# Two units' keys turned by VectorE and GpSimd instead of by TensorE

## The chip, the cores and the metric

The kernel runs on one core of a Trainium2 chip. The metric is the device time of one execution in microseconds (us); a kernel is told by the median of its runs. Of the profile and the trace, times are microseconds from the first instruction unless marked ns. Engines are called PE (TensorE), DVE (VectorE), ACT (ScalarE), POOL (GpSimd) and SP (SyncE, which here issues transfers).

## The reference

A gated linear attention (4 batches, 8 heads, 768 positions, head size 48) feeds a two-layer network with a squared ReLU (3072 tokens, 384 by 2048 by 384), all in float32.

```python
f = 1.0 / (1.0 + np.exp(-f_logit))
for t in range(S):
    state = f[:, :, t, :, None] * state + np.einsum('bhd,bhe->bhde', k[:, :, t], v[:, :, t])
    y[:, :, t] = np.einsum('bhd,bhde->bhe', q[:, :, t], state)
x = np.ascontiguousarray(attn_out.transpose(0, 2, 1, 3)).reshape(B * S, H * D)
h = x @ w_in
r = np.maximum(h, 0.0)
return (r * r) @ w_out
```

## The kernel before, in words

**Attention.** The 768 positions are cut into 6 blocks of 128 (`TB`), each of two chunks of 64 (`C`). A unit is one pair of heads in one block for all four batches; there are 24, numbered from 0, four to a block: unit 8 is the first of block 2, units 10 and 12 are the third of block 2 and the first of block 3. The fourth unit of a block (11, 15, ...) has no inputs of its own: it works on rows that the other three hand over (`last_kq`, `last_kn`). A unit goes through lettered stages, run by `stage`: `L` loads f, k and q (one tile `fkq`, three tiles in turn), `v` loads the values, `G` is the sigmoid on ACT, `K` scans the gates backwards on DVE and scales the keys, with two small limits on POOL, `Q` scans forwards and scales the queries, `T` turns the keys (tokens to rows) by four PE transposes into a PSUM tile `shared`, and `N` lets ACT copy them to `kn` and a strip of them to `last_kn`. Units 13, 14 and later ones do `B` in the place of `T`: DVE transposes every 32 by 32 block of the keys (`STREAM_TRANSPOSE`), and POOL moves the blocks to their mirrored places by 16 copies; the keys then stand in SBUF and no copy to `kn` is needed.

**Network.** Blocks go through the network in 16 steps each (one per 128 hidden features): `up` is nine PE products into a bank `ph`, `square` is three ACT operations, `rest` a DVE subtraction that gives `gl`, and `down`, two steps later, nine products into three sums `po`. When a block's last `down` is done, `finish` copies the three sums out (ACT, DVE, ACT; `ob`) and SP sends each to DRAM. `flow` runs these steps in one row, numbered n: block 1 in steps 0 to 15, the rest of block 0 in 16 to 25, block 2 from 26.

**What sets the order.** `hook(n, place, ...)` hangs the attention's stages into step n: place 0 is ahead of `up`, 0.5 and 0.7 are around `rest`, 1 is behind `down`. `SLOTS` says after which step a unit's own PE work comes (unit 8: 13, 9: 16, 10: 19, 11: 21, 12: 23, 13: 27), and the tables `STAGE_AT` and `BLOCKS_AT` give the other stages relative to that step. PE, DVE, ACT and SP execute in the order in which the program is written; only POOL's order is chosen by a scheduler when the program is built.

**The slot.** `slot(old, new)` mixes the old unit's outputs with the new unit's scores and state updates on PE. All updates go to the one bank `shared`, the first chunk's (rows 0 to 63) early and the second chunk's (rows 64 to 127) last. Between them stands a tick: a POOL `MEMSET` of one word (`flag`) that waits for the last update of the first chunk, and that the first update of the second chunk waits for:

```python
if c == 0 and b == B - 1 and h:
    seen.append(G.memset(tick, 0).ins)
    behind(seen[0], ins)
elif c and b == 0 and h:
    behind(ins, seen[0])
```

Each engine executes in its own order, so whatever stands ahead of a tick on POOL also stands ahead of the second half of that slot on PE.

Of the kernel before, what the change touches and what calls it, by code (L numbers as in the profile page):

```python
# [13 lines left out]
F32 = mybir.dt.float32  # L14
F32R = mybir.dt.float32r
# [7 lines left out]
P = 128  # L23
B, H, S, D = 4, 8, 768, 48
# [6 lines left out]
NT = B * TB  # L31
# [10 lines left out]

LAG = 2
Q = 32
TURNED = 13
AHEAD = 4
LO = 6
SPLIT = 2
# [9 lines left out]

SLOTS = (13, 16, 19, 21, 23, 27, 31, 35, 39, 43, 47, 51, 55, 59, 63, 67, 71)
STAGE_AT = ((-6, 0, "Lv"), (-3, 1, "GK"), (-1, 0.5, "Q"), (-1, 1, "TN"), (1, 1, "s"))  # L60
BLOCKS_AT = ((-6, 0, "Lv"), (-3, 1, "GKB"), (-1, 0.5, "Q"), (0, 0.7, "N"), (1, 1, "s"))
LAST_AT = ((-6, 0, "v"), (1, 1, "s"))


# [291 lines left out]
    return t.rearrange("p (n t) -> p n t", t=C)  # L356


def scanned(t):
    return t.rearrange("p (n t) -> p n t", t=CZ)  # L360


def fast_path(ctx, psum, tc, moe, ident, low, flag, fkqT, vN, w, w4, out):
    nc = tc.nc
    V, G = nc.vector, nc.gpsimd
# [17 lines left out]
    for r in (0, C):  # L383
        G.affine_select(
            out=mask[r : r + C], in_=mask[r : r + C], compare_op=ALU.is_ge, fill=0.0,
# [19 lines left out]
    class Unit:  # L405
# [36 lines left out]
        def gates(self):  # L442
            nc.scalar.activation(scanned(self.fz[:, 1:])[:, :, :C], chunks(self.ft), AF.Sigmoid)  # L443

        def keys(self):

            rr = self.rr
            V.tensor_tensor_scan(  # L448
                out=rr[:, ::-1], data0=self.fz[:, NZ * CZ : 0 : -1], data1=dr[:, ::-1], initial=0.0,
                op0=ALU.mult, op1=ALU.add,  # L450
            )
            for pe, of in ((self.pe, rr[:, ::CZ]), (low[:, self.t], self.pe)):
                G.tensor_scalar(out=pe, in0=of, scalar1=LOWEST, scalar2=None, op0=ALU.max)  # L453
            V.tensor_tensor(
                out=chunks(self.kt), in0=chunks(self.kt), in1=scanned(rr)[:, :, 1:], op=ALU.mult
            )
# [54 lines left out]
                    out=self.pk[:, b], in_=self.kt[:, b * TB : (b + 1) * TB], identity=ident  # L511
                )

        def turn_blocks(self):


            if self.n < 14:
                both = self.wk([P, 2, NT], "ys")
                kb, kn = both[:, 0], both[:, 1]
            else:  # L520
                kb, kn = (
                    moe.gp.tile([P, NT], F32, tag=f"part{i}", name=f"turn{self.nm}_{i}", bufs=1) for i in range(2)
                )
            V.transpose(out=kb, in_=self.kt)  # L524
            kb, self.kn = (t.rearrange("p (b n) -> p b n", b=B) for t in (kb, kn))
            self.pk = self.kn
            for a in range(0, P, Q):
                for r in range(0, P, Q):
                    G.tensor_copy(out=self.kn[a : a + Q, :, r : r + Q], in_=kb[r : r + Q, :, a : a + Q])  # L529

        def turned(self):
            if self.n < TURNED:
                self.kn = self.wk([P, B, ROWS], "kn")
                nc.scalar.copy(out=self.kn, in_=self.pk[:, :, :ROWS])
            at = self.hp * (C - D)
            nc.scalar.copy(
                out=last_kn.rearrange("p b (h r) -> p b h r", h=2)[:, :, :, at : at + C - D],
                in_=self.pk.rearrange("p b (h r) -> p b h r", h=2)[:, :, :, D:],
            )
# [100 lines left out]
        def upper(self):  # L640

            self.x = self.xs[self.blk]
            y = self.x[self.hp] if self.own else self.wk([ROWS, 2, NT], "ys", 1, F32R)
            if not self.own:
                self.x.append(y)
            self.y = [y[:ROWS, i].rearrange("p (b c t) -> p c b t", b=B, c=NC) for i in range(2)]
            self.py = self.py[:ROWS].rearrange("p c (b t) -> p c b t", t=C)
            nc.scalar.copy(out=self.y[0], in_=self.py)  # L648
# [26 lines left out]
        def stage(self, letters):  # L675
            for c in letters:
                {
                    "L": lambda: self.load(slice(0, 3)),
                    "f": lambda: self.load(slice(0, 1)),
                    "k": lambda: self.load(slice(1, 2), slice(2, 3)),  # L680
                    "v": lambda: self.load_v(),
                    "G": lambda: self.gates(),
                    "K": lambda: self.keys(),
                    "Q": lambda: self.queries(),
                    "m": lambda: self.move(),
                    "r": lambda: self.crossed(),
                    "T": lambda: self.turn(),
                    "B": lambda: self.turn_blocks(),
                    "N": lambda: self.turned(),
                    "D": lambda: self.add(),  # L690
                    "S": lambda: self.scores(),
                    "M": lambda: self.masked(),
                    "C": lambda: self.states(),
                    "s": lambda: self.crossed_states(),
                    "Y": lambda: self.outputs(),
                    "H": lambda: self.upper(),
                    "z": lambda: self.less(),
                    "X": lambda: self.lower(),
                    "g": lambda: self.parts((1,), G if self.blk < 2 else nc.sync),
                    "h": lambda: self.parts((0,), nc.sync),  # L700
                }[c]()
# [7 lines left out]
    )  # L709
    half = list(range(LO)), list(range(LO, NF))  # L710
    xs = {blk: moe.new_x(blk, blk) for blk in range(2)}
    units, decoding, shared = {}, {}, []

    for t in xs[0]:
        G.memset(t[C + 32 :].bitcast(F32), 0.0)
# [10 lines left out]
    def slot(old, new):  # L726

        ab = ps_a.tile([P, 2, 512], F32, tag="ab", name=f"ab{(new or old).nm}_{new is None}")
        rows = [[], []]
        if old:
            old.py = ab[:, :, : B * C]
            for c in range(NC):
                for b in range(B):
                    for part in range(2):
                        for h in (c, 1 - c):
                            rows[c].append((C, lambda a=(part, b, c, h): old.output_one(*a)))
        if new:  # L740
            new.sd = ab[:, :, B * C :]
            new.dd = shared[0].rearrange("p (c e) n -> p c (e n)", c=NC)[:, :, : B * D]
            adds = [
                [] if new.last_of(c) else [
                    (D, lambda a=(b, c, h): update(*a)) for b in range(B) for h in (c, 1 - c)
                ] for c in range(NC)
            ]
            for h in range(2):
                for b in range(B):
                    for c in (h, 1 - h):  # L750
                        rows[h].append((C, lambda a=(b, c, h): new.score_one(*a)))
            rows = [adds[0] + rows[0], rows[1] + adds[1]]
        seen = []

        def behind(ins, first):
            tc.add_manual_dep(ins, first.name, mybir.DependencyInfo(
                mybir.DependencyClass.Sync, mybir.DependencyReason.DATA
            ), reason="one bank")

        def update(b, c, h):  # L760
            ins = new.add_one(new.dd, b, c, h).ins
            if c == 0 and b == B - 1 and h:

                seen.append(G.memset(tick, 0).ins)  # L764
                behind(seen[0], ins)
            elif c and b == 0 and h:
                behind(ins, seen[0])

        at = [0, 0]
        while any(rows):  # L770
            r = min((r for r in range(2) if rows[r]), key=lambda r: at[r])
            cols, do = rows[r].pop(0)
            at[r] += cols
            do()
# [51 lines left out]
    with tc.manual_schedule(engines={ET.PE, ET.SP, ET.DVE, ET.Activation}):  # L826
# [21 lines left out]
        def hook(n, at, do):  # L848
            hooks.setdefault((max(n, 0), at), []).append(do)

        def third():
            early.close()
            moe.inputs(ctx)
            xs[2] = moe.new_x(2, 2)

# [3 lines left out]
        for n in range(1, NF - 1):  # L861
# [23 lines left out]
            hook(n, 0.5, after)  # L885
            hook(n, 0.7, last)
        hook(NF - 1, 0, third)
        late = [Unit(n, xs, (ps_a,)) for n in range(2 * HP, NBLK * HP)]
        for at, old, un in zip(SLOTS, (None, *late), (*late, None)):
            if un:  # L890
                for n, place, stage in LAST_AT if not un.own else STAGE_AT if un.n < TURNED else BLOCKS_AT:
                    hook(at + n, place, lambda un=un, stage=stage: un.stage(stage))
            hook(at, 1, lambda old=old, un=un: slot(old, un))
            if old:
                hook(at, 1, lambda old=old: old.stage("HX" if old.own else "HXhg"))
            if un:
                hook(at, 1, lambda un=un: un.stage("rMCm" if un.own else "rMC"))
# [238 lines left out]
```

## Time and profile before

| | |
|---|---|
| median of 3 runs | 483.72 us (483.42 to 485.64) |
| profiled execution | 485.02 us, of which the span from first to last instruction is 483.2 |
| granted PE clock, mean | 0.985 of full speed |
| PE busy | 467.4 us, 97% of the span |
| ACT, DVE, POOL busy | 277.7, 261.8 and 80.0 us |
| PE, four transposes of one late unit | line L510, into `shared`, 16 of them (units 8, 9, 10, 12) |

"Busy" is the share of the span in which an engine executes; PE's products are pipelined, so the distance from one start to the next is the better measure of what a product costs. A line such as L244 is line 244 of the kernel before. In a timeline, equal instructions that follow each other are merged into one row with their count, and a bracket tells how long the engine was idle and what ended that.

### The profile page before, as it was taken

Reading aid. Unit: us, or ns where it says so; the run is one execution under the profiler, and the core shown is the slowest. Engines: PE = TensorE matmul, PEld = TensorE weight load, DVE = VectorE, ACT = ScalarE, POOL = GpSimd, SP = SyncE. Lnnn points to the kernel's source line nnn. Section 1 sums busy time; section 2 is a strip of 40 time slices with the busy share of each in tenths; the row PEclk is TensorE's granted clock in tenths of the full one; section 3 lists DMA queues with packets and bytes.
Section 4 is the critical chain, followed back from the end, with each engine's and each line's share of the span. In section 5 each row is a group of like instructions: output and inputs, shape, how many; then the busy total and the mean of one; then the engine's idle time right before and its main releaser. Section 6 shows DMA issues by size and latency. Waiting matters only on the chain. (4 is left out here: it accounts for less than half of the span.)

```text
span 483.2 us, 11552 instructions
## 1 busy us (share of the span) xinstructions
PE 467.4 (97%) x4763; PEld 384.8 (80%) x4763; DVE 261.8 (54%) x482; ACT 277.7 (57%) x562; POOL 80.0 (17%) x210
## 2 busy tenths in 40 slices
PE   5889999999999999999999999999999999999996
PEld 4767788888888888888888888888888888888884
DVE  7998885889966557543447453356353312221111
ACT  4687666877857565545546645555654543544441
POOL 6122010001010004150053250052350000000000
PEclk8699999999999999999999999999999999999999
DMA  8985316568104205332005332004300002100002
GB/s 290 308 248 139 102 41 228 170 208 288 32 14 157 84 3 125 95 94 81 3 2 125 96 93 84 1 1 111 108 12 3 2 0 34 66 0 2 1 0 71
DMA packets 22636, 42.60 MB, mean 88 GB/s; under 512 B 4512, under 2 KB 8128, under 8 KB 22576
## 3 DMA queue, kind: packets, MB, share of 16 engines
q1 hardware_dynamic: 22128, 40.86, 27.8%
q0 software_dynamic: 448, 0.92, 0.8%
q8 instruction: 39, 0.64, 0.5%
q14 instruction: 21, 0.17, 0.1%
HBM read 31.69 MB, written 4.72 MB: 75 GB/s over the span
## 5 line engine op out<-in xcount | busy, mean ns | idle before, releaser
L244 PE MATMUL ph<-x,w 128*128 128x512 f32 x864 | 214.9, 393 | 0.0
L244 PEld LDWEIGHTS ph<-x,w 128*128 128x128 f32 x864 | 160.0, 188 | 34.2 <-DVE gl L261 0.3
L271 PE MATMUL po<-gh,w 128*128 128x512 f32 x570 | 175.5, 389 | 0.0
L261 DVE TENSOR_TENSOR gl<-ph,gh 128x512 fp32r<-128x512 f32 x95 | 65.4, 688 | 158.8 <-ACT gh L256 158.6
L254 ACT ACTIVATE ph<-ph 128x512 f32<-128x512 f32 x96 | 55.9, 582 | 125.2 <-PE ph L244 124.9
L271 PEld LDWEIGHTS po<-gh,w 128*128 128x128 f32 x570 | 107.0, 188 | 22.2
L271 PE MATMUL po<-gl,w 128*128 128x512 f32 x285 | 111.1, 390 | 0.0
L271 PEld LDWEIGHTS po<-gl,w 128*128 128x128 f32 x285 | 53.5, 188 | 11.2
L255 ACT ACTIVATE ph<-ph 128x512 f32<-128x512 f32 x96 | 55.9, 582 | 3.0
L256 ACT CAST gh<-ph 128x512 fp32r<-128x512 f32 x95 | 55.8, 587 | 3.0
L529 POOL COPY turn<-turn 32x128 f32<-32x128 f32 x112 | 42.1, 376 | 8.3 <-DVE turn L524 3.7
L453 POOL TENSOR_SCALAR fkq<-fkq 128x8 f32<-128x8 f32 x18 | 12.9, 717 | 144.9 <-DVE fkq L448 122.1
L448 DVE TENSOR_TENSOR_SCAN fkq<-fz,dr 128x520 f32<-128x520 f32 x18 | 22.3, 1238 | 7.2 <-ACT fz L443 7.2
L169 ACT CAST w<-wa 128x384 fp32r<-128x384 f32 (+1 forms) x33 | 16.6, 513 | 15.4 <-DVE wa L156 11.7
L462 DVE TENSOR_TENSOR_SCAN fkq<-fz,dz 128x520 f32<-128x520 f32 x18 | 22.4, 1246 | 0.6
L619 PE MATMUL ab_False<-sc,vn 64*48 64x64 f32 (+1 forms) x480 | 20.7, 220 | 0.0
L141 ACT ACTIVATE wa<-raw 128x384 f32<-128x384 f32 (+1 forms) x33 | 18.1, 549 | 4.0 <-DMA raw<-in_w_dram 3.9
L664 DVE TENSOR_TENSOR x<-ab_False,x 112x512 fp32r<-112x512 f32 x12 | 8.3, 692 | 21.7 <-ACT x L648 21.7
L648 ACT CAST x<-ab_False 112x512 fp32r<-112x512 f32 x12 | 7.0, 587 | 22.5 <-PE shared L554 17.6
L628 PE MATMUL ab_False<-rx,sx 48*48 48x64 f32 (+1 forms) x240 | 19.4, 216 | 0.0
L764 POOL MEMSET flag<- 1x1 int32 x16 | 1.4, 88 | 106.2 <-PE shared L554 104.3
L152 DVE SCALAR_TENSOR_TENSOR wa<-raw,wa 128x384 int32<-128x384 int32 (+1 forms) x33 | 18.0, 552 | 0.7
(148 smaller groups left out, 494.0 us busy)
## 6 DMA issues: line engine op xcount, KB each, us to landing
raw<-in_w_dram SPq DMA_DIRECT2D x32, 384.0 KB, 4.2
fkq<-in_fkqT_dram SPq DMA_DIRECT2D x15, 768.0 KB, 5.9
vn<-in_vN_dram SPq DMA_DIRECT2D x24, 192.0 KB, 4.7
out_dram<-ob SPq DMA_DIRECT2D x14, 256.0 KB, 2.2
fkq<-in_fkqT_dram SPq DMA_DIRECT2D x9, 256.0 KB, 4.8
x<-ys SPq DMA_DIRECT2D x30, 64.0 KB, 2.4
last_kq<-fkq SPq DMA_DIRECT2D x28, 64.5 KB, 2.3
out_dram<-part SPq DMA_DIRECT2D x3, 256.0 KB, 2.2
```

The costliest lines, as they stand in the source:

```text
L141: nc.scalar.activation(a, upper_f, AF.Abs, scale=2.0**-112, **kw)
L244: self.nc.tensor.matmul(self.cur.ph[f], lhsT=w[:, i], rhs=x[:, j], start=first and n == 0, stop=last and n == 2)
L254: nc.scalar.activation(ph, ph, AF.Relu)
L255: nc.scalar.activation(ph, ph, AF.Square)
L256: nc.scalar.copy(out=gh, in_=ph)
L261: self.nc.vector.tensor_tensor(out=gl, in0=self.cur.ph.pop(f), in1=gh.bitcast(F32), op=ALU.subtract)
L271: self.nc.tensor.matmul(c.po[e], lhsT=l, rhs=r, start=f == c.fs[0] and i == 0, stop=f in c.ends and i == 2, skip_group_check=len(c.ends) > 1,)
L448: V.tensor_tensor_scan(out=rr[:, ::-1], data0=self.fz[:, NZ * CZ : 0 : -1], data1=dr[:, ::-1], initial=0.0, op0=ALU.mult, op1=ALU.add,)
L462: V.tensor_tensor_scan(out=pp, data0=self.fz[:, : NZ * CZ], data1=dz, initial=0.0, op0=ALU.mult, op1=ALU.add)
L529: G.tensor_copy(out=self.kn[a : a + Q, :, r : r + Q], in_=kb[r : r + Q, :, a : a + Q])
L619: nc.tensor.matmul(to[:m], lhsT=self.vn[rows, b, h * D : h * D + m], rhs=self.sc[rows, h, b], start=b == 0, stop=none and c == 0 and b == ...
L628: nc.tensor.matmul(to[:m], lhsT=s[rows, b * D : b * D + m], rhs=q[rows], start=False, stop=b == B - 1,)
```

## The change

Units 10 and 12 now turn their keys by DVE's block transpose and POOL's 16 copies as the later ones do; only units 8 and 9 still use PE in this part. `turn_blocks` is split into `blocks` (`b`, the DVE transpose) and `turn_blocks` (`B`, the POOL copies). Unit 10 writes into the tile that will later hold the third input row group of block 2 (`x2`), unit 12 into `ys`. Unit 10's other stages stay where they were. Unit 12 gets a table of its own, `EARLY_AT`: its load moves from place 0 to place 1 of step 17, and its sigmoid and keys move up from step 20 to step 18; its copies come after slot 19. The copies are told to the scheduler as standing behind the tick of the slot before them.

```diff
-BLOCKS_AT = ((-6, 0, "Lv"), (-3, 1, "GKB"), (-1, 0.5, "Q"), (0, 0.7, "N"), (1, 1, "s"))
+BLOCKS_AT = ((-6, 0, "Lv"), (-3, 1, "GKbB"), (-1, 0.5, "Q"), (0, 0.7, "N"), (1, 1, "s"))
+EARLY_AT = (
+    (-6, 1, "Lv"), (-5, 1, "GKb"), (-4, 1, "B"), (-1, 0.5, "Q"), (0, 0.7, "N"), (1, 1, "s")
+)
...
-        def turn_blocks(self):
+        def blocks(self):
...
             if self.n < 14:
-                both = self.wk([P, 2, NT], "ys")
-                kb, kn = both[:, 0], both[:, 1]
+                kb, kn = halved(
+                    self.wk([P, 2, NT], "ys") if self.blk > 2 else
+                    moe.xs[2].tile([P, 2, NT], F32, tag="x2", name=f"turn{self.nm}")
+                )
...
             V.transpose(out=kb, in_=self.kt)
-            kb, self.kn = (t.rearrange("p (b n) -> p b n", b=B) for t in (kb, kn))
+            self.kb, self.kn = (t.rearrange("p (b n) -> p b n", b=B) for t in (kb, kn))
             self.pk = self.kn
+
+        def turn_blocks(self):
+
             for a in range(0, P, Q):
                 for r in range(0, P, Q):
-                    G.tensor_copy(out=self.kn[a : a + Q, :, r : r + Q], in_=kb[r : r + Q, :, a : a + Q])
+                    ins = G.tensor_copy(
+                        out=self.kn[a : a + Q, :, r : r + Q], in_=self.kb[r : r + Q, :, a : a + Q]
+                    ).ins
+                    for t in ticks[-1:]:
+                        tc.add_manual_dep(ins, t.name, mybir.DependencyInfo(
+                            mybir.DependencyClass.NoSync, mybir.DependencyReason.SCHED_ONLY
+                        ), reason="behind the last slot")
 
         def turned(self):
-            if self.n < TURNED:
+            if self.n < 10:
...
+        def stages_of(un):
+            if not un.own:
+                return LAST_AT
+            return STAGE_AT if un.n < 10 else EARLY_AT if un.n == 12 else BLOCKS_AT
```

What that makes of the order is seen at three places. Line numbers are those of the kernel shown, so the same code has a higher number in the changed kernel; `fkq_2`, `turn_2` belong to unit 10, `fkq_0`, `ys_0` to unit 12.

**POOL, around slot 19, before.** The first `MEMSET` is the tick of slot 16, the next that of slot 19, the last two those of slots 21 and 23.

```order
L764 MEMSET flag 1x1
L453 TENSOR_SCALAR fkq_2_1763<-fkq_2_1763 128x8
L453 TENSOR_SCALAR low<-fkq_2_1763 128x8
L764 MEMSET flag 1x1
L453 TENSOR_SCALAR fkq_0_2033<-fkq_0_2033 128x8
L453 TENSOR_SCALAR low<-fkq_0_2033 128x8
L764 MEMSET flag 1x1 x2
```

The same place in the changed kernel:

```order
L785 MEMSET flag 1x1
L460 TENSOR_SCALAR fkq_2_1763<-fkq_2_1763 128x8
L460 TENSOR_SCALAR low<-fkq_2_1763 128x8
L541 COPY turn_2_2031<-turn_2_2031 32x4x32 x16
L460 TENSOR_SCALAR fkq_0_2085<-fkq_0_2085 128x8
L460 TENSOR_SCALAR low<-fkq_0_2085 128x8
L785 MEMSET flag 1x1
L541 COPY ys_0_2125<-ys_0_2125 32x4x32 x16
L785 MEMSET flag 1x1 x2
```

Unit 10's copies and unit 12's two limits on its keys now stand ahead of the tick of slot 19.

**SP, steps 16 to 21, before.** These are the transfers that SP issues, in order: the rows handed over by units 8 and 9, the load of unit 12, the three outputs of block 1, the rows of unit 10.

```order
L473 DMA last_kq<-fkq_1_1632 16x1032 x2
L436 DMA fkq_0_2033<-in_fkqT_dram 128x3x512
L440 DMA vn_0_2035<-in_vN_dram 128x384
L336 DMA out_dram<-ob_0_2062 128x512
L336 DMA out_dram<-ob_1_2065 128x512
L336 DMA out_dram<-ob_2_2068 128x512
L473 DMA last_kq<-fkq_2_1763 16x1032 x2
```

The same place in the changed kernel:

```order
L480 DMA last_kq<-fkq_1_1632 16x1032 x2
L338 DMA out_dram<-ob_0_2074 128x512
L338 DMA out_dram<-ob_1_2077 128x512
L338 DMA out_dram<-ob_2_2080 128x512
L443 DMA fkq_0_2085<-in_fkqT_dram 128x3x512
L447 DMA vn_0_2087<-in_vN_dram 128x384
L480 DMA last_kq<-fkq_2_1763 16x1032 x2
```

The load of unit 12 moved behind the three outputs.

**DVE, steps 17 to 19, before.** Each scan stands here as `SCALAR_TENSOR_TENSOR` (in the trace `TENSOR_TENSOR_SCAN`); `ob_1` is the second output copy.

```order
L448 SCALAR_TENSOR_TENSOR fkq_2_1763<-fz_71,dr 128x520
L454 TENSOR_TENSOR fkq_2_1763<-fkq_2_1763 128x512
L261 TENSOR_TENSOR gl_7_2048<-ph_7_2037,gh_7_2047 128x512
L335 COPY ob_1_2065<-po_0_1_1320 128x512
L460 RECIPROCAL dz<-fkq_2_1763 128x8
L462 SCALAR_TENSOR_TENSOR fkq_2_1763<-fz_71,dz 128x520
L465 TENSOR_TENSOR fkq_2_1763<-fkq_2_1763 128x512
L261 TENSOR_TENSOR gl_8_2084<-ph_8_2073,gh_8_2083 128x512
L261 TENSOR_TENSOR gl_9_2122<-ph_9_2111,gh_9_2121 128x512
```

The same place in the changed kernel:

```order
L461 TENSOR_TENSOR fkq_2_1763<-fkq_2_1763 128x512
L533 STREAM_TRANSPOSE turn_2_2031<-fkq_2_1763 128x512
L263 TENSOR_TENSOR gl_7_2060<-ph_7_2049,gh_7_2059 128x512
L337 COPY ob_1_2077<-po_0_1_1320 128x512
L467 RECIPROCAL dz<-fkq_2_1763 128x8
L469 SCALAR_TENSOR_TENSOR fkq_2_1763<-fz_71,dz 128x520
L472 TENSOR_TENSOR fkq_2_1763<-fkq_2_1763 128x512
L263 TENSOR_TENSOR gl_8_2100<-ph_8_2089,gh_8_2099 128x512
L455 SCALAR_TENSOR_TENSOR fkq_0_2085<-fz_72,dr 128x520
L461 TENSOR_TENSOR fkq_0_2085<-fkq_0_2085 128x512
L533 STREAM_TRANSPOSE ys_0_2125<-fkq_0_2085 128x512
L263 TENSOR_TENSOR gl_9_2138<-ph_9_2127,gh_9_2137 128x512
```

Unit 10's transpose came in ahead of the output copy `ob_1`, and unit 12's keys came in ahead of `gl_9`. On ACT the sigmoid of unit 12 now stands behind `gh_8`, ahead of the ReLU of step 19, and the two copies to `kn` are gone.

## Rows read from the trace of the kernel before

**Rows 1.** Page, busy time, share of the span and instructions of each engine.

```profile
PE 467.4 (97%) x4763; PEld 384.8 (80%) x4763; DVE 261.8 (54%) x482; ACT 277.7 (57%) x562; POOL 80.0 (17%) x210
```

**Rows 2.** Timeline of PE, end of step 18: start us, us, instruction, count.

```profile
150.18 0.39 PE L271 MATMUL po<-gl,w 128*128 128x512 f32 x1
...
152.26 0.60 PE L510 MATMUL shared<-ident,fkq 128*128 128x128 f32 x4
152.61 2.33 PE L244 MATMUL ph<-x,w 128*128 128x512 f32 x9
154.78 0.39 PE L271 MATMUL po<-gl,w 128*128 128x512 f32 x1
```

**Rows 3.** Timeline of PE, second half of slot 19, steps 20 and 21.

```profile
158.34 0.20 PE L554 MATMUL shared<-vn,kn 64*48 64x48 f32 x1
...
161.01 0.39 PE L271 MATMUL po<-gl,w 128*128 128x512 f32 x1
...
163.05 2.20 PE L244 MATMUL ph<-x,w 128*128 128x512 f32 x9
165.09 0.39 PE L271 MATMUL po<-gl,w 128*128 128x512 f32 x1
```

**Rows 4.** Timeline of PE, transposes of unit 12.

```profile
173.35 0.60 PE L510 MATMUL shared<-ident,fkq 128*128 128x128 f32 x4
173.70 2.31 PE L244 MATMUL ph<-x,w 128*128 128x512 f32 x9
```

**Rows 5.** Timeline of DVE: unit 10's keys, output copy, a scan, unit 13's transpose.

```profile
148.69 0.69 DVE L454 TENSOR_TENSOR fkq<-fkq 128x512 f32<-128x512 f32 x1
...
149.90 0.68 DVE L335 COPY ob<-po 128x512 f32<-128x512 f32 x1
...
164.48 1.24 DVE L448 TENSOR_TENSOR_SCAN fkq<-fz,dr 128x520 f32<-128x520 f32 x1 [0.74 <-ACT fz L443]
...
187.56 0.71 DVE L524 STREAM_TRANSPOSE ys<-fkq 128x512 f32<-128x512 f32 x1
188.20 0.69 DVE L261 TENSOR_TENSOR gl<-ph,gh 128x512 fp32r<-128x512 f32 x1
```

**Rows 6.** Timeline of SP's issues: load of unit 12, second and third output.

```profile
143.59 0.60 SPq L436 DMA_DIRECT2D fkq<-in_fkqT_dram  x1
...
150.61 0.81 SPq L336 DMA_DIRECT2D out_dram<-ob  x2
```

**Rows 7.** DMA view, loads issued at 158.45, 210.86, 143.59, 115.87; last column: us to landing.

```profile
fkq<-in_fkqT_dram SPq DMA_DIRECT2D x1, 768.0 KB, 4.8
...
fkq<-in_fkqT_dram SPq DMA_DIRECT2D x1, 768.0 KB, 4.6
...
fkq<-in_fkqT_dram SPq DMA_DIRECT2D x1, 768.0 KB, 6.4
...
fkq<-in_fkqT_dram SPq DMA_DIRECT2D x1, 768.0 KB, 8.2
```

**Rows 8.** Timeline of ACT: a unit's sigmoid.

```profile
163.82 0.63 ACT L443 ACTIVATE fz<-fkq 128x512 f32<-128x512 f32 x1
```

**Rows 9.** Timeline of POOL: tick of slot 19, unit 12's limits, unit 13's copies.

```profile
157.58 0.09 POOL L764 MEMSET flag<- 1x1 int32 x1 [7.78 <-PE shared L554]
165.81 0.74 POOL L453 TENSOR_SCALAR fkq<-fkq 128x8 f32<-128x8 f32 x1 [8.14 <-DVE fkq L448]
166.63 0.23 POOL L453 TENSOR_SCALAR low<-fkq 128x8 f32<-128x8 f32 x1
...
188.41 6.74 POOL L529 COPY ys<-ys 32x128 f32<-32x128 f32 x16 [0.47 <-DVE ys L524]
```

**Rows 10.** Windows: us, busy us of each engine (instructions), PEclk, DMA share, GB/s.

```profile
8.10:21.70 13.60, 10.44 (x209) 8.67 (x213) 12.95 (x21) 8.78 (x23) 3.76 (x8) 0.50 1.05 347
...
38.00:42.00 4.00, 2.98 (x71) 2.29 (x70) 3.67 (x6) 2.79 (x6) 0.95 (x2) 1.00 0.22 42
```

**Rows 11.** Timeline of PE, first transposes of the program.

```profile
7.42 0.66 PE L510 MATMUL pk<-ident,fkq 128*128 128x128 f32 x4 [2.36 <-DVE fkq L454]
```

More of the change, by code (lines that the diff above doesn't have):

```diff
@@ L44 @@
 Q = 32
-TURNED = 13
 AHEAD = 4
@@ L356, in chunks, with halved @@
     return t.rearrange("p (n t) -> p n t", t=C)
+def halved(t):
+    t = t.rearrange("p a n -> p (a n)")
+    return t[:, :NT], t[:, NT:]
 def scanned(t):
@@ L642, in upper @@
             self.x = self.xs[self.blk]
+            if self.blk == 2 and self.own:
+                self.x.append(moe.xs[2].tile([P, 2, NT], F32R, tag=f"x{self.hp}", name=f"x2_{self.hp}"))
             y = self.x[self.hp] if self.own else self.wk([ROWS, 2, NT], "ys", 1, F32R)
@@ L687, in stage @@
                     "T": lambda: self.turn(),
+                    "b": lambda: self.blocks(),
                     "B": lambda: self.turn_blocks(),
@@ L711, in fast_path @@
     xs = {blk: moe.new_x(blk, blk) for blk in range(2)}
-    units, decoding, shared = {}, {}, []
+    units, decoding, shared, ticks = {}, {}, [], []
     for t in xs[0]:
@@ L764, in update @@
                 seen.append(G.memset(tick, 0).ins)
+                ticks.append(seen[0])
                 behind(seen[0], ins)
@@ L853, in third @@
             moe.inputs(ctx)
-            xs[2] = moe.new_x(2, 2)
+            xs[2] = []
         hook(0, 0.5, rest_of_first)
@@ L888, in fast_path @@
         late = [Unit(n, xs, (ps_a,)) for n in range(2 * HP, NBLK * HP)]
+        def stages_of(un):
+            if not un.own:
+                return LAST_AT
+            return STAGE_AT if un.n < 10 else EARLY_AT if un.n == 12 else BLOCKS_AT
         for at, old, un in zip(SLOTS, (None, *late), (*late, None)):
             if un:
-                for n, place, stage in LAST_AT if not un.own else STAGE_AT if un.n < TURNED else BLOCKS_AT:
+                for n, place, stage in stages_of(un):
                     hook(at + n, place, lambda un=un, stage=stage: un.stage(stage))
```

## Prediction

> **What bounds the kernel now.** I read the page's busy times first, then PE's timeline step by step. PE is busy for 97% of the span, no other engine for more than 57% [rows 1], so the question at every edit is what it takes from PE and whether PE has to wait for it. PE's starts then show how tightly it runs: from one `down` to the next `up` and on to the next `down` are 2.04 us each (161.01 to 163.05 to 165.09), nine products with no hole [rows 3]. In steps 16 to 23, where the change lies, PE waits for nothing. So PE's own work there is worth its full length, and any new wait costs its full length too. The slots are the only places in this part where PE depends on POOL: the second chunk's updates of slot 19 start at 158.34 [rows 3], and the tick that they need was written at 157.58 [rows 9], after 7.78 us in which POOL did nothing but wait for PE.
>
> **What is removed.** Unit 10's four transposes stand between 152.26 and 152.61: 0.35 us. The `up` behind them takes 2.17 (to 154.78), 0.13 more than the plain 2.04, and the `down` ahead of them 2.08 (150.18 to 152.26), 0.04 more [rows 2, 3]. Together 0.52 us. Unit 12's stand from 173.35 to 173.70, again 0.35 [rows 4]; with the same 0.13 behind them that is 0.48. Sum: 1.00 us off PE. The bound below it is the bare 0.70, if the slower neighbours have another cause. The two copies to `kn` go from ACT, which is not what PE waits for, and count nothing.
>
> **What is added off the path.** Two DVE transposes of 0.71 each, with the next instruction 0.64 after [rows 5], and twice 16 POOL copies, 6.74 per unit [rows 9]. Unit 10's: its scaled keys end at 149.38 (148.69 + 0.69), the transpose would start at 149.42 and end at 150.13, the copies run from about 150.3 to 157.0. The first chunk's updates need only the eight copies into rows 0 to 63, which are done before 156.4, where slot 19 will now begin; the second chunk's come at 157.8. So these copies stay hidden, but with 0.8 us to spare: if they were that much later they would stall PE directly. Unit 12's copies come behind the tick of slot 19 and have until slot 23. The two tiles lent for the blocks are written again only after slots 21 and 23, behind the updates that read them; that costs nothing while PE's order holds.
>
> **What is moved, and whom it makes wait.** Unit 12's load now stands on SP behind the three outputs, and unit 12's two limits stand on POOL ahead of the tick of slot 19. That ties slot 19 to a load. I follow it through.
>
> The second output waits for DVE's copy `ob_1`, which started at 149.90 and ended at 150.58 [rows 5]; SP issued it at 150.61 [rows 6]. With unit 10's transpose ahead of it, keys end 149.38, transpose from 149.42, `gl_7` from 150.06, `ob_1` from 150.66 to 151.34. SP issues outputs two and three from 151.37 and needs 0.81 us for both [rows 6], so unit 12's load goes out at about 152.2; before, it went out at 143.59 [rows 6].
>
> A load of this size (768 KB) that ran alone landed 4.8 and 4.6 us after its issue; the one issued at 143.59 took 6.4, and one issued at 115.87, beside the weight loads, 8.2 [rows 7]. I take 4.8, since the outputs ahead are short and nothing else is under way: it lands at 157.0.
>
> The sigmoid takes 0.63 [rows 8], to 157.65. The scan starts then; POOL's first limit starts 1.33 us after the start of a scan (164.48 to 165.81), the second 0.82 later, and that one lasts 0.23 [rows 5, 9]. So the first starts at 159.0, the second ends at 160.1, and the tick is written at about 160.2, where PE would be ready for it at 157.82 (158.34 less the 0.52 gained). PE waits about 2.4 us in the middle of slot 19. Behind the stopped update on PE stand the rest of slot 19 and everything after it, so nothing covers this.
>
> Sum: + 2.43 - 1.00 = + 1.4 us. With the load at 4.6 us it is + 1.2; at 6.4 us, + 3.0; at 8.2 us, + 4.8; with the transposes at their lower bound 0.3 more.
>
> For the load there is a rule: the Trainium skill, "DMA: Bandwidth & Descriptors", section "Anatomy of one DMA", puts a transfer at a fixed 2.0 us plus its bytes over 436 GB/s, by its own account fitted for another issuing path. For 768 KB that is an estimate of 3.8 us, by which the wait would be 1.4 and the sum + 0.4. The trace does not bear it out, since the two loads alone took 4.6 and 4.8 [rows 7].
>
> What is late next: ACT has the sigmoid ahead of the ReLU of step 19, which would start at 157.7. Its `gl_9` would then end by 161.2, and PE needs that bank for the `up` of step 21, which starts only after 165. DVE's and POOL's following work has as much room. I count no second wait.
>
> **The forecast.** The profiled execution took 485.02 us and would take 486.4; the median of the runs lies 1.30 below that execution. 483.72 + 1.43 gives 485.2 us, 0.3% slower. About 0.5% (2.4 us) is what a measurement of this kernel can tell from no change, so I count this as within it.
>
> **The rivals.**
>
> A: PE's wait costs the clock. The granted clock was 0.50 from 8.1 to 21.7 us [rows 10], and shortly before it fell PE had stood idle for 2.36 us, until 7.42 [rows 11]; the wait that I expect is as long. Against it: between 38 and 42 us PE was busy for only 2.98 of 4 us, and the clock stayed at 1.00 [rows 10]; and unlike at the start, dense products stand before and behind this wait. At half clock, PE loses half of the stretch: 6.8 us if it lasted 13.6 us as it did there, but then PE was fed poorly; with its work at hand I take a quarter to a half of that, 1.7 to 3.4. It decides from 1.0 us on, since 1.4 + 1.0 passes the bound. The time would be 486.9 to 488.6. The Trainium skill, "TensorE: Matmul & The Clock Gate", section "Why this matters for your kernels", warns of idle gaps between bursts of products in the middle of a kernel for this reason. The trace agrees for the gap at the start and shows no such gap later.
>
> B: the load is slow. The three outputs' bytes are still moving when it is issued, or something else is. At 6.4 to 8.2 us to landing [rows 7] the time is 486.7 to 488.5. Against it: outputs are a third of its size each and nothing else is due.
>
> C: PE does not wait, and only the removed transposes count: 483.72 - 1.0 = 482.7 us. That asks for a tick at 157.8, so for a load that lands at 154.6, 2.4 us after its issue. Nothing of this size came near that [rows 7]; it could happen only if SP issued the load 2.4 us sooner than I work out, so if `ob_1` were not late and the outputs went out at once.
>
> **How the numbers follow.** The forecast gets 0.52 (its own range is 484.9 to 486.1, loads of 4.6 to 5.5 us), A 0.28, B 0.08, C 0.10, a gain past 2.4 us by something that I do not see 0.02. Within 0.5% are the forecast and C, 0.62, less 0.03 for a wait at its upper end: 0.59. Slower are A, B and that end: 0.39. The range leaves out C below and the ends of A and B above: 484.4 to 488.6.
>
> **What would show it.** In the changed kernel's trace: `up` directly behind `down` at the ends of steps 18 and 22, with 2.04 us each; unit 12's load issued at about 152.2, landing near 157; the sigmoid waiting for that landing; POOL's two limits behind the scan, then the tick; and in the wait view a PE wait for POOL's `flag` of about 2.4 us in slot 19, a single one. Wrong would be: no such wait (C), a wait of more than 3.5 us (B), a granted clock of 0.50 in the slices behind slot 19 (A), or a wait at the start of slot 19 for the copies, or at the `up` of step 21 for `gl_9`.

## The result and the profile after

The changed kernel takes 487.49 us (median of 6 runs, 486.71 to 488.03), the kernel before 483.69 beside it (6 runs, 483.38 to 485.64): a ratio of 1.0068, 95% interval 1.0054 to 1.0082. It is slower, by 0.68% as that ratio has it (3.3 us); the two medians differ by 3.8 us. I had forecast 1.4 us and "within 0.5%". The time lies in my range and in the intervals of rivals A and B.

The profiled execution took 488.03 us, with a span of 486.3. PE is busy 1.2 us longer than before [rows 1], although 8 of its 4763 instructions are gone; POOL is busy 11 us longer. The page:

```profile
PE 468.6 (96%) x4755; PEld 384.9 (79%) x4755; DVE 263.2 (54%) x484; ACT 277.3 (57%) x560; POOL 91.0 (19%) x242
```

I measure the change by one stretch, from the first product of slot 16 to the first of slot 27, since the edit lies inside it. It is 54.43 us long before (142.01 to 196.44) and 57.13 after (141.95 to 199.08): 2.70 more. The rest agrees to 0.06 up to the start of the last `down`; from there to the end it took 13.02 us before and 13.43 after. That 0.4 us belongs to the change too: the tail is 13.0 in the kernel before and in those below with one unit turned (e2, e3), and 13.4 to 13.5 in all eleven traces with both. All of it lies behind the last output copy, where the program closes (3.20 us before, 3.62 after); what takes it there stays open. Below I compare the stretch; the tail comes on top of it.

The view of PE's waits names two in this stretch, where before there was none:

```profile
PE shared L572 <- POOL flag L785: 2.7, 1, 2.7
PE po L273 <- DVE ob L337: 0.3, 1, 0.3
```

Columns are us in total, times, and the longest. PE's timeline shows both in place, and answers to [rows 2, 3]:

```profile
150.12 0.39 PE L273 MATMUL po<-gl,w 128*128 128x512 f32 x1
150.35 0.61 PE L273 MATMUL po<-gh,w 128*128 128x512 f32 x2
151.30 0.50 PE L273 MATMUL po<-gl,w 128*128 128x512 f32 x1 [0.34 <-DVE ob L337]
...
152.80 2.21 PE L246 MATMUL ph<-x,w 128*128 128x512 f32 x9
154.84 0.39 PE L273 MATMUL po<-gl,w 128*128 128x512 f32 x1
...
161.39 0.25 PE L572 MATMUL shared<-vn,turn 64*48 64x48 f32 x2 [2.68 <-POOL flag L785]
161.90 2.37 PE L246 MATMUL ph<-x,w 128*128 128x512 f32 x9
164.10 0.40 PE L273 MATMUL po<-gl,w 128*128 128x512 f32 x1
```

From the top: the `down` of step 18 stops before its second sum, and lasts 2.68 us (150.12 to 152.80) instead of 2.08. The `up` behind it starts with no transposes between and takes 2.04. In slot 19 the second chunk's updates wait 2.68 us for the tick; the slot, which began at 156.97, lasts 4.92 us to the `up` at 161.90, where it had lasted 1.92. That is 3.00 more, since the trace counts a wait from the end of the product ahead, and products overlap. So the stretch is +0.60 + 3.00 - 0.95 (what the transposes gave back), about +2.7.

The long wait is followed back through the other engines' timelines and the issue view. POOL, where the tick is the `MEMSET` [rows 9]:

```profile
150.21 6.66 POOL L541 COPY turn<-turn 32x128 f32<-32x128 f32 x16 [0.47 <-ACT sx L490]
160.40 0.59 POOL L460 TENSOR_SCALAR fkq<-fkq 128x8 f32<-128x8 f32 x1 [3.54 <-DVE fkq L455]
161.07 0.23 POOL L460 TENSOR_SCALAR low<-fkq 128x8 f32<-128x8 f32 x1
161.25 0.09 POOL L785 MEMSET flag<- 1x1 int32 x1
161.77 5.47 POOL L541 COPY ys<-ys 32x128 f32<-32x128 f32 x16 [0.43 <-DVE ys L533]
```

DVE [rows 5] and ACT [rows 8]:

```profile
149.36 0.71 DVE L533 STREAM_TRANSPOSE turn<-fkq 128x512 f32<-128x512 f32 x1
150.00 0.65 DVE L263 TENSOR_TENSOR gl<-ph,gh 128x512 fp32r<-128x512 f32 x1
150.57 0.68 DVE L337 COPY ob<-po 128x512 f32<-128x512 f32 x1
...
158.93 1.24 DVE L455 TENSOR_TENSOR_SCAN fkq<-fz,dr 128x520 f32<-128x520 f32 x1 [4.79 <-ACT fz L450]
```

```profile
158.26 0.63 ACT L450 ACTIVATE fz<-fkq 128x512 f32<-128x512 f32 x1 [6.13 <-DMA fkq<-in_fkqT_dram]
```

SP's issues [rows 6], and from the DMA view the load of unit 12 with its us to landing [rows 7]:

```profile
148.90 3.20 SPq L338 DMA_DIRECT2D out_dram<-ob  x3
152.20 0.62 SPq L443 DMA_DIRECT2D fkq<-in_fkqT_dram  x1
152.86 0.64 SPq L447 DMA_DIRECT2D vn<-in_vN_dram  x1
153.60 1.15 SPq L480 DMA_DIRECT2D last_kq<-fkq  x2
```

```profile
fkq<-in_fkqT_dram SPq DMA_DIRECT2D x1, 768.0 KB, 6.0
```

Read backwards: the tick at 161.25 stands behind the two limits, these behind the scan of 158.93, that behind the sigmoid of 158.26, that behind a load issued at 152.20. POOL had its 16 copies done at 156.87 and then waited 3.54 us with the tick in its queue, although the first chunk's updates, which alone the tick needs, were done by 158.71, when PE fell idle.

### The profile page after: what moved, and what is told of

It is laid out like the page before. It is cut to its first block, busy times and chain, and to the rows that moved or that the text cites. A ratio compares the mean times of both kernels' runs of the same rounds, so it can differ in the third digit from the quotient of the medians.

```text
span 486.3 us, 11573 instructions
## 1 busy us (share of the span) xinstructions
PE 468.6 (96%) x4755; PEld 384.9 (79%) x4755; DVE 263.2 (54%) x484; ACT 277.3 (57%) x560; POOL 91.0 (19%) x242
## 5 line engine op out<-in xcount | busy, mean ns | idle before, releaser
L246 PEld LDWEIGHTS ph<-x,w 128*128 128x128 f32 x864 | 160.2, 188 | 35.0 <-DVE w L173 0.8
L541 POOL COPY turn<-turn 32x128 f32<-32x128 f32 x128 | 48.3, 377 | 9.7 <-DVE turn L533 4.0
```

The source lines that it names most:

```text
L246: self.nc.tensor.matmul(self.cur.ph[f], lhsT=w[:, i], rhs=x[:, j], start=first and n == 0, stop=last and n == 2)
L541: ins = G.tensor_copy(out=self.kn[a : a + Q, :, r : r + Q], in_=self.kb[r : r + Q, :, a : a + Q]).ins
```

## The experiments

The theories: **T1**, the loss is PE's waits, one for the load through limits and tick, one for the output copy behind unit 10's transpose. **T2**, the turning on DVE and POOL costs PE time by itself. **T3** (rival A), the idle of slot 19 lowers PE's clock behind it. All are read on the same stretch, 54.43 us before. Ratios are to the kernel before on the same chip.

### e1: the load of unit 12 ahead of the outputs

```diff
-    (-6, 1, "Lv"), (-5, 1, "GKb"), (-4, 1, "B"), (-1, 0.5, "Q"), (0, 0.7, "N"), (1, 1, "s")
+    (-6, 0, "Lv"), (-5, 1, "GKb"), (-4, 1, "B"), (-1, 0.5, "Q"), (0, 0.7, "N"), (1, 1, "s")
```

> Only the load of unit 12 goes back to place 0 of step 17, ahead of the three outputs. If the wait in slot 19 comes from that load by way of the two limits ahead of the tick (the main theory), the load lands at about 150, the limits are done right behind unit 10's copies at 158.0, and PE waits 0 to 0.2 us there in place of 2.68; what is left is +0.6 us for the output copy that comes late to the down of step 18 and -1.0 us for the eight transposes: 483.3 us. If the rival holds (POOL is simply late with unit 10's 16 copies, slowed by DVE), the load changes nothing: a wait of about 2.7 us and 486.5 us or more.

484.51 us, ratio 1.0014 (0.9998 to 1.0029); stretch 54.57. The load was issued at 143.03 and landed at 147.88, and of the long wait 0.16 us was left, in a slot of 2.40; the `down` of step 18 stayed at 2.68. That is T1, with one surprise that made it 0.5 us longer than I expected. POOL:

```profile
149.71 7.94 POOL L541 COPY turn<-turn 32x128 f32<-32x128 f32 x16 [0.47 <-ACT sx L490]
157.73 0.24 POOL L460 TENSOR_SCALAR fkq<-fkq 128x8 f32<-128x8 f32 x1
158.05 0.23 POOL L460 TENSOR_SCALAR low<-fkq 128x8 f32<-128x8 f32 x1
158.23 0.09 POOL L785 MEMSET flag<- 1x1 int32 x1
```

The 16 copies now take 7.94 us instead of 6.66, and limits and tick come right behind them. Most single copies take 0.29 us; one that meets a scan of DVE takes 1.1 to 1.2, and the next, which meets the scaling behind the scan, 0.75. With unit 12's keys early, a second scan runs beside the copies. The Trainium skill, "SBUF — State Buffer", section "SBUF: two separate sides", says why: VectorE and GpSimd share one pair of SBUF ports, held for a whole instruction, also by a VectorE instruction with two SBUF inputs. The trace agrees: the copy that met unit 12's scan ended at 154.87, the scan at 154.78.

### e2 and e3: one unit alone

e2 leaves unit 10 to PE, e3 unit 12.

e2:

```diff
-            if self.n < 10:
+            if self.n < 11:
...
-            return STAGE_AT if un.n < 10 else EARLY_AT if un.n == 12 else BLOCKS_AT
+            return STAGE_AT if un.n < 11 else EARLY_AT if un.n == 12 else BLOCKS_AT
```

e3:

```diff
-            if self.n < 10:
+            if self.n < 10 or self.n == 12:
...
-            return STAGE_AT if un.n < 10 else EARLY_AT if un.n == 12 else BLOCKS_AT
+            return STAGE_AT if un.n < 10 or un.n == 12 else BLOCKS_AT
```

> Unit 10 is turned by PE again; unit 12 stays as in the change, its load behind the outputs. Main theory: the tick still stands behind the limits that wait for the load, which goes out 0.7 us sooner (no DVE transpose ahead of the output copy), so PE waits about 2.2 us in slot 19; no 0.6 us in step 18; -0.5 us for unit 12's transposes: 485.4 us. Rival (unit 10's copies hold the tick): no copies, no wait, 483.2 us.

> Unit 12 is back as before (PE transposes, load and keys in their old places); unit 10 as in the change. Main theory: no limits of unit 12 ahead of the tick, so no wait in slot 19 beyond 0.2 us; the down of step 18 still takes about 0.6 us more since the output copy stands behind unit 10's DVE transpose; -0.5 us for unit 10's transposes: 483.8 us, no change. Rival (copies): the wait of 2.7 us stays and the time is about 486.4 us.

e2: 487.39 us, ratio 1.0054 (1.0031 to 1.0076). No wait in step 18, and a wait of 1.75 us in slot 19, which lasted 3.99. But the stretch is 57.71, not some 56: behind that wait PE's clock fell. Columns of a window: us, busy us of PE, PEld, DVE, ACT and POOL with their instructions, granted clock, DMA share, GB/s.

```profile
161.50:164.90 3.40, 3.40 (x10) 2.64 (x9) 2.32 (x6) 1.53 (x4) 2.98 (x11) 0.50 0.35 132
```

The `up` there took 3.13 us and the `down` 2.73, 1.65 us over the usual 2.17 and 2.04. Without that it would be 56.06, as expected. That was the first sign of T3, and behind an idle shorter than the 2.68 of the changed kernel's first trace, where the clock had stayed.

e3: 484.13 us, ratio 1.0004 (0.9992 to 1.0016). No wait in slot 19, only that of the `down` of step 18 (2.67); stretch 54.56, 0.13 over before. The transposes of unit 10 give back 0.48, its wait takes 0.59. So the 16 copies cost PE nothing, and the turn of unit 10 still gains nothing.

### e5: the tick ahead of the limits, with the load still late

Unit 12's two limits become a stage of their own behind slot 19, and the scheduler is told to put them behind the tick.

```diff
-    (-6, 1, "Lv"), (-5, 1, "GKb"), (-4, 1, "B"), (-1, 0.5, "Q"), (0, 0.7, "N"), (1, 1, "s")
+    (-6, 1, "Lv"), (-5, 1, "GKb"), (-4, 1, "lB"), (-1, 0.5, "Q"), (0, 0.7, "N"), (1, 1, "s")
...
-            for pe, of in ((self.pe, rr[:, ::CZ]), (low[:, self.t], self.pe)):
-                G.tensor_scalar(out=pe, in0=of, scalar1=LOWEST, scalar2=None, op0=ALU.max)
+            if self.n != 12:
+                self.limits()
...
+        def limits(self):
+
+            for pe, of in ((self.pe, self.rr[:, ::CZ]), (low[:, self.t], self.pe)):
+                ins = G.tensor_scalar(out=pe, in0=of, scalar1=LOWEST, scalar2=None, op0=ALU.max).ins
+                for t in ticks[-1:] if self.n == 12 else ():
+                    tc.add_manual_dep(ins, t.name, mybir.DependencyInfo(
+                        mybir.DependencyClass.NoSync, mybir.DependencyReason.SCHED_ONLY
+                    ), reason="behind the last slot")
...
```

> The load stays late, behind the outputs; only POOL's order is changed: unit 12's two limits stand behind the tick of slot 19 (they are issued in a step of their own). Main theory: PE no longer depends on the load, the wait in slot 19 is gone (below 0.3 us), the sigmoid still waits about 6 us for the load without anybody on PE feeling it: +0.6 -1.0, 483.3 us. Rival (copies, or PE needs the load in another way): the wait stays near 2.7 us, 486.5 us or more.

484.26 us, ratio 0.9995 (0.9982 to 1.0009); stretch 54.07, 0.36 under before. The load landed at 157.55, as late as in the changed kernel, and ACT waited 5.85 us for it; but POOL:

```profile
157.22 0.09 POOL L795 MEMSET flag<- 1x1 int32 x1 [0.78 <-PE shared L581]
159.62 0.68 POOL L468 TENSOR_SCALAR fkq<-fkq 128x8 f32<-128x8 f32 x1 [2.32 <-DVE fkq L455]
```

The tick waits for PE alone, and slot 19 lasts 1.92. This is the plainest of the runs: a late load harms only through what stands ahead of the tick.

### e4: one more load ahead of unit 12's

512 KB into a tile not in use, issued by SP just ahead, with the tick held behind the limits as in the changed kernel.

```diff
-    (-6, 1, "Lv"), (-5, 1, "GKb"), (-4, 1, "B"), (-1, 0.5, "Q"), (0, 0.7, "N"), (1, 1, "s")
+    (-6, 1, "2Lv"), (-5, 1, "GKb"), (-4, 1, "B"), (-1, 0.5, "Q"), (0, 0.7, "N"), (1, 1, "s")
...
+        def spare_load(self):
+            spare = moe.xs[2].tile([P, 2, NT], F32, tag="x1", name=f"spare{self.nm}")
+            nc.sync.dma_start(spare, fkqT[self.blk, self.hp, :, 0:2])
...
```

> The change, with 512 KB more loaded into an unused tile ahead of unit 12's load, and POOL's order held as in the change (limits ahead of the tick). If PE's wait follows the landing of the load (main theory), the load lands about 1.5 us later and the wait in slot 19 grows from 2.68 to about 4.2 us: from the start of slot 16 to the start of slot 27 58.6 us (57.1 in the change, 54.4 before), or about 2 us more where the clock falls behind the wait, which I expect in most runs of this kernel. If POOL's copies made the wait, it would stay at 2.7 us.

490.29 us, ratio 1.0122 (1.0103 to 1.0141). The wait in slot 19 grew to 3.23 us, not to 4.2: the load was issued 0.53 us behind the spare one and landed after 6.13. So the direction is T1's, but half a megabyte more ahead of it hardly delays a load. The clock fell here too, to 0.50 for 6.8 us, and the stretch was 60.26.

### e6 and e7: the output copy away from DVE

e6 lets ACT make all three output copies of block 1; e7 is e6 with e5's limits.

```diff
-                (nc.vector.tensor_copy if e % 2 else nc.scalar.copy)(out=ob, in_=c.po[e])
+                (nc.vector.tensor_copy if e % 2 and c.blk != 1 else nc.scalar.copy)(out=ob, in_=c.po[e])
```

> The change, with all three output copies of block 1 made by ACT, so that none stands behind unit 10's DVE transpose. Theory: the 0.34 us hole and the 0.6 us in the down of step 18 go, and the outputs and unit 12's load go out 1.8 us sooner, so the wait in slot 19 falls from 2.68 to about 1.4 us: 55.3 us from slot 16 to slot 27. Rival for the 0.6 us (the network's products simply run slower beside POOL's copies): the down of step 18 stays at 2.68 us.

> Unit 12's limits behind the tick, and the output copies of block 1 by ACT. Both waits gone, only the eight transposes less: 53.4 us from slot 16 to slot 27, 1.0 us less than before, and a time 1.0 us (0.2%) below that of the kernel before. If a third wait had been hidden behind the two, it would show here.

e6: 484.45 us, ratio 1.0012 (0.9994 to 1.0030); stretch 55.25. PE, from the `down` of step 18 to the `up` behind it:

```profile
149.70 0.39 PE L273 MATMUL po<-gl,w 128*128 128x512 f32 x1
...
151.74 2.20 PE L246 MATMUL ph<-x,w 128*128 128x512 f32 x9
```

The `down` is back at 2.04, so the copy on DVE was what it had waited for. The outputs go out sooner, the load is issued 8.4 us behind the start of slot 16 instead of 10.3, and the wait in slot 19 is 1.45.

e7: 484.21 us, ratio 0.9994 (0.9976 to 1.0012); stretch 54.11 where I expected 53.4. Both waits are gone, and a third is there, 0.33 us in a slot of 2.57:

```profile
154.30 7.99 POOL L550 COPY turn<-turn 32x128 f32<-32x128 f32 x16 [0.47 <-ACT ob L337]
162.35 0.09 POOL L795 MEMSET flag<- 1x1 int32 x1
```

As in e1, unit 12's earlier scan lengthens the copies, and the tick stands right behind them. That the whole time gains nothing is as the stretch (0.32 under before) and the tail (0.4 over) have it.

### e9: unit 12's load and keys where they stood before

e6's copies on ACT, and unit 12's stages back at their places of before; the copies come behind the tick of slot 21.

```diff
-    (-6, 1, "Lv"), (-5, 1, "GKb"), (-4, 1, "B"), (-1, 0.5, "Q"), (0, 0.7, "N"), (1, 1, "s")
+    (-6, 0, "Lv"), (-3, 1, "GKb"), (-2, 1, "B"), (-1, 0.5, "Q"), (0, 0.7, "N"), (1, 1, "s")
```

> Both units' keys are turned by DVE and POOL, but unit 12's load and keys stand where they stood before the change (load in step 17 at place 0, keys in step 20, copies behind the tick of slot 21), and ACT makes all three output copies of block 1, so that no output copy stands behind unit 10's transpose. My theory (all of the loss is two waits, each made by what was put ahead of something that PE needs; the turning itself costs PE nothing): slot 19 is 1.9 us long without a wait, the `down` of step 18 takes 2.04, unit 10's sixteen copies take 6.7 us since no scan runs beside them, and from the start of slot 16 to the start of slot 27 it is 53.4 to 53.5 us, 0.95 to 1.0 under the kernel before; the time is about 0.2% below before, too little to tell it from no change with certainty. Rival 1 (turning on DVE and POOL slows PE by itself, by work beside it): the stretch is 54.2 us or more although there is no wait. Rival 2 (a third wait comes from DVE, since unit 12's scan, keys and transpose stand in one row in step 20 ahead of that step's `gl`): a PE idle of 0.2 to 0.7 us behind step 21 or 22.

483.56 us, ratio 0.9988 (0.9974 to 1.0003); stretch 53.44, as worked out. POOL:

```profile
148.29 6.69 POOL L541 COPY turn<-turn 32x128 f32<-32x128 f32 x16 [0.47 <-ACT ob L337]
155.07 0.09 POOL L785 MEMSET flag<- 1x1 int32 x1
163.38 0.68 POOL L460 TENSOR_SCALAR fkq<-fkq 128x8 f32<-128x8 f32 x1 [8.21 <-DVE fkq L455]
164.14 0.23 POOL L460 TENSOR_SCALAR low<-fkq 128x8 f32<-128x8 f32 x1
165.37 0.09 POOL L785 MEMSET flag<- 1x1 int32 x1 [1.00 <-PE shared L572]
165.80 6.84 POOL L541 COPY ys<-ys 32x128 f32<-32x128 f32 x16 [0.34 <-issue]
```

Nothing of unit 12 stands ahead of the first tick, and PE waits for nothing in the whole stretch. T2 falls: both units are turned on DVE and POOL, and PE's stretch is shorter by the full 0.99 us of the removed transposes. The tail gives 0.4 us of that back. On the whole time the median is 0.2% lower, and the interval still reaches 1: this version is better than the changed kernel, and against the kernel before only the stretch shows a gain.

### e8, e10, e11, e12: the changed kernel again

The kernel unaltered, in four more executions with a trace.

> The change itself once more, beside the others on one chip. Wait in slot 19 of 2.2 to 3.5 us with the load's landing, 0.6 us in step 18, 57 us from slot 16 to slot 27 where the clock stays up, about 1.7 us more where it falls: a ratio to the kernel before of 1.006 to 1.009.

> The changed kernel unaltered, for a third look at its clock behind slot 19 (granted clock 1.00 in the first execution, 0.50 for 3.5 us in the second). If the fall of the clock explains what is left of the difference of the medians (3.8 us against 2.7 us in the steps), the products behind slot 19 run at 0.50 in most of these looks, slots 16 to 27 then take 58.0 to 59.5 us, and with the clock up 57.1. If the first execution was the rule, the clock stays at 1.00 here.

> The same once more, the fourth look: 58.0 to 59.5 us from slot 16 to slot 27 with the clock at 0.50 behind slot 19, 57.1 us with it at 1.00.

> The same once more, the fifth look: 58.0 to 59.5 us from slot 16 to slot 27 with the clock at 0.50 behind slot 19, 57.1 us with it at 1.00. A fall in none of the three would leave the 1.1 us open.

e8: 488.39 us, ratio 1.0088 (1.0066 to 1.0111). The other three took 489.39, 489.15 and 490.41, one execution each, and the kernel before 484.31 beside them. The waits repeat: 2.67 to 2.69 us for the `down` of step 18, and 2.37 to 2.49 of idle in slot 19. The clock does not: windows of the first execution, then of e8, e11 and e12 behind that idle:

```profile
161.40:164.80 3.40, 3.40 (x39) 2.80 (x40) 2.86 (x7) 1.91 (x4) 2.66 (x10) 1.00 0.51 195
```

```profile
160.40:163.90 3.50, 3.50 (x33) 2.80 (x31) 2.75 (x7) 1.39 (x3) 2.90 (x10) 0.51 0.49 187
```

```profile
161.80:164.90 3.10, 3.10 (x8) 2.43 (x8) 2.53 (x7) 1.19 (x3) 2.73 (x10) 0.50 0.31 114
```

```profile
161.00:167.20 6.20, 6.20 (x39) 4.92 (x40) 3.41 (x8) 2.54 (x5) 4.82 (x16) 0.50 0.32 121
```

e10 is like e11 (0.50 from 162.0 to 165.2). What that does is seen on e12's PE:

```profile
160.93 0.32 PE L572 MATMUL shared<-vn,turn 64*48 64x48 f32 x2 [2.37 <-POOL flag L785]
161.78 4.21 PE L246 MATMUL ph<-x,w 128*128 128x512 f32 x9
165.78 0.63 PE L273 MATMUL po<-gl,w 128*128 128x512 f32 x1
...
168.59 2.20 PE L246 MATMUL ph<-x,w 128*128 128x512 f32 x9
```

The `up` takes 4.00 us instead of 2.17 and the `down` 2.81 instead of 2.04. The stretches are 58.43 (e8), 58.36, 58.54 and 59.71 against 57.13 with the clock up. T3 holds in four of the five executions with a trace. Over all the kernels, the clock fell in six of the seven traces in which the idle of slot 19 is 1.75 us or more, and in none of the seven in which it is 1.45 or less, that of before among them.

With the tail, the five executions cost 4.4 us on the mean (58.43, 4.0 over before, and 0.4), and 3.1 with the clock up; the medians differ by 3.8 in the first measurement and by 4.1 in e8. So the fall is part of the loss. In how many of the executions without a trace it came isn't shown.

## Why the prediction came out as it did

**Right.** The transposes' 1.00 us came back (0.95, and 0.99 in e9). Both units' copies off the path: yes in the changed kernel, and with "0.8 us to spare": lengthened by 1.3 us, they held the tick in e1 and e7. Unit 12's load at "about 152.2": 152.20. The chain from landing to sigmoid, scan, limits and tick, and a wait of "about 2.4 us" for `flag` in slot 19: 2.37 to 2.68. e5 and e1 show that it needs both, the late load and the limits ahead of the tick. Nobody waited for `gl_9`.

**Mis-sized.** "I take 4.8" for the load: it took 5.7 to 6.0, so the tick came at 161.25, not 160.2. The reason I gave, that nothing else was under way, missed the two `last_kq` transfers, which SP issues 1.4 us behind the load and which themselves took 5.4 and 5.0 us to land, where those issued at 139.42 and 139.99 had taken 2.4 and 2.3. That they slowed the load is not shown. With them 2.5 us behind it, it took 5.0 in e7, but in e6 the sigmoid that waits for it started 6.07 us after its issue; with none issued while it was under way, it took 6.4 before [rows 7] and 6.3 in e9, but 4.8 in e1. What set its time stays open. That PE's wait was nevertheless as forecast is luck: PE too was late, by the next point.

**Failed: "I count no second wait".** I had worked out that unit 10's transpose pushes the copy `ob_1` from 149.90 to 150.66, and asked only what SP would do with it. The same copy frees the bank of the second sum, and the `down` of step 18 is the first of the next pass into these sums. Its second part started at 150.86 before, and the copy ended at 150.58 [rows 5]: 0.28 us of room.

```profile
150.86 0.39 PE L271 MATMUL po<-gl,w 128*128 128x512 f32 x1
```

In the changed kernel that part was due at 150.80 (150.12 plus a third of 2.04), and the copy ended at 151.25, 0.67 later than before. It started at 151.30, 0.50 late, and the first product took 0.11 longer. The cost, 0.60 here and 0.59 in e3, is gone in e6. So are there, and in e9, the 0.04 us by which that `down` exceeded 2.04 before; unit 12's transposes had no such 0.04 ahead of them, so I should not have booked it to those of unit 10.

**Failed: the likeliest case.** I took the clock as staying up and gave rival A 0.28; it came in four of the five executions with a trace. I let the window at 38 to 42 us, busy for 2.98 of 4 us at 1.00 [rows 10], speak against it, but its gap is 1.02 us long; the fall in the trace of before that followed a gap of over 2 us [rows 10, 11] was the nearer row. The same gap is longer in the traces of e4 and e7, and there the clock fell. The gap before, then those of e4 and e7 with a window behind each:

```profile
39.80 0.36 PE L628 MATMUL py<-rx,sx 48*48 48x64 f32 x3 [1.02 <-DMA rx<-fkq]
```

```profile
40.98 0.46 PE L652 MATMUL py<-rx,sx 48*48 48x64 f32 x3 [2.12 <-DMA rx<-fkq]
41.00:44.30 3.30, 3.30 (x56) 2.89 (x57) 1.29 (x3) 1.44 (x4) 0.80 (x2) 0.50 0.04 9
```

```profile
41.32 0.46 PE L655 MATMUL py<-rx,sx 48*48 48x64 f32 x3 [2.31 <-DMA rx<-fkq]
41.00:47.60 6.60, 6.28 (x77) 4.87 (x79) 2.66 (x5) 3.09 (x8) 1.99 (x5) 0.50 0.18 32
```

These two executions took 494.02 and 489.14 us, 3.7 and 4.9 over the medians of their kernels. The warning of the Trainium skill, "TensorE: Matmul & The Clock Gate", section "Why this matters for your kernels", which I had named beside A, pointed the right way, although the idles here are shorter than the gaps it warns of. My price for it, 1.7 to 3.4 us, was near: 1.5 to 2.9, by the four stretches against 57.13 less the 0.2 to 0.3 us by which their waits were shorter. Together: + 2.4 - 1.0 was forecast; on the stretch about + 2.7 with the clock up, and + 3.9 to + 5.3 where it fell, were measured, and 0.4 in the tail, which I had not seen.

Rival B's slow load of 6.4 us or more did not come, and C's absent wait needed another order (e3, e5 or e9). My range held because it took in A and B, not by the likeliest case.

## What to carry to other kernels

Whatever stands ahead of a signal on an in-order engine is part of what its waiter waits for: a load that "has time" had none, once its consumer's consumer was queued ahead of a tick, and two instructions put behind the tick took all of that wait away (e5). When an instruction is inserted ahead of a copy out of PSUM, ask for every reader of that copy's end, the next writer of the bank as much as the output. And price an idle of PE by more than its length: one of 2.4 us cost another 1.5 to 2.9 us in four of five traces, and one trace can miss that.

## What the runs showed of the hardware

The granted clock fell to 0.50, the lower of the two levels, behind idles in slot 19 of 1.75 (e2), 2.37 to 2.49 (e8, e10, e11, e12) and 3.23 us (e4), although dense products stood before and behind them, and behind 2.12 (e4) and 2.31 us (e7) near 39 us; it stayed at 1.00 behind 2.68 us in one execution and behind 1.45 (e6). So the length of the idle alone did not decide it; what else did is open. Sixteen POOL copies took 5.4 to 5.5 us with no DVE scan beside them (unit 12's in the first trace and in e6), 6.6 to 6.8 with one scan and its scaling, and 7.9 to 8.0 with two (e1, e7).
